# Unit 0's angles moved ahead of unit 1's gates, part of the gate arithmetic on other engines, and a new set of due times, in a gated linear attention with routed experts

## The chip, the cores and the metric

One core of one Trainium2 chip runs the whole program. The metric is the device time of one execution in microseconds. A profiled execution gives the trace; its span is what lies between the program's first and last instruction. The engines are named as in the profile: PE (TensorE matmuls), PEld (its weight loads), DVE (VectorE), ACT (ScalarE), POOL (GpSimd) and SP (the queue that issues most DMAs).

## The reference

The first half is a linear attention with a complex gate, over B = 4 batches, H = 8 heads, S = 768 positions, D = 48, all in float32:

```python
mag = np.sqrt(a_re * a_re + a_im * a_im)
scale = np.minimum(mag, 0.999) / (mag + 1e-06)
a_re_n, a_im_n = (a_re * scale, a_im * scale)
for t in range(S):
    ar, ai = (a_re_n[:, :, t, :, None], a_im_n[:, :, t, :, None])
    new_re = ar * S_re - ai * S_im
    new_im = ar * S_im + ai * S_re
    kv = np.einsum('bhd,bhe->bhde', k[:, :, t], v[:, :, t])
    S_re, S_im = (new_re + kv, new_im)
    y[:, :, t] = np.einsum('bhd,bhde->bhe', q[:, :, t], S_re)
```

The second half takes y as 3072 rows of 384, chooses the best of 8 experts for each row with `w_gate`, and gives each row its gate value times `relu(x @ w1[e]) @ w2[e]`.

## The kernel before

**Units and batches.** The sequence is cut into six units of 128 positions, which lie on the partitions. A unit has four batches; the loop `for g in range(NT)` runs over the 24 pairs (unit, batch). A half is two of a unit's four batches.

**The gates of a unit** become a decay and an angle. `gate_steps` makes four steps of the data `ar`, `ai`: `s0` a lower bound (a ScalarE Relu, or a VectorE maximum where `c<unit>` is true) and Ln; `s1` Exp, the ratio `ai*R` (L222), its clipping (L223) and its square (L224); `s2` Ln and a sum; `s3` Exp and the final log decay. `decay` sums that over the positions with a triangular matmul (`csl`) and takes two exponentials, E and Ei, for q and for k. `angle` takes the arctangent, `turns` sums it with matmuls (`cst`) and reduces it to whole and broken turns (`fg`, L283 to L286), and `rotation` takes two sines (`CS`). For units 2 to 4, `angle` also adds the phase carried from the unit before, which goes through DRAM (`cd`, `carry`). `csl` and `cst` share one PSUM buffer (`psC`).

**Attention.** `products` forms `Qe = q*E`, `Ke = k*Ei` and from them Q and K of 96 columns a head. `scores` transposes K and Q on TensorE (`tp`), ScalarE copies them out (`kt`, `qt`), TensorE multiplies (`at`), VectorE masks (`am`). `outer` forms K'V (`dk`), `state` updates the state `G` on VectorE. `results` sums, in one PSUM tile `yt`, `am` times V and, for units after the first, `qt` times `G`; `evict` copies `yt` to `ys`, `finish` turns it back to rows (`xb`), writes `x` to DRAM (`xd`) and keeps the router's logits. After units 2, 4 and 5 `route` ranks the rows for the experts.

**Experts.** From about 271 us on the eight experts follow one after another, each with its gathered rows, two matmul chains and a scatter.

**Order.** Instructions are placed by a planner: `put(t, f)` gives what `f` emits a due time `t`, counted in batches (lower is earlier), and an engine's ready instructions go in by due time. The times stand in the table `WHEN`: `s1.0.2` is step 2 of unit 1's part 0, `d` a decay, `a` an angle, `t` turns, `r` a rotation, `w` a group of `warm` matmuls (of no use to the result, they keep TensorE running), `p<n>` how many of unit n+1's gate steps are traced ahead of unit n's sine table. Unit 0 is done in three parts: batch 0, batch 1, batches 2 and 3.

**Two ScalarE tables.** Ln and Exp need one table, arctangent and sine the other. `table` loads one (`LE<n>`, `TR<n>`, about 1.28 us) and is ordered behind every table function traced since the last load, and every later one behind it. In the kernel before, unit 1's steps 0 and 1 are traced ahead of TR0 and its arctangent under TR0 too; the last two steps of unit 0's part 2 and unit 1's steps 2 and 3 follow LE1, and with them all four steps of unit 2.

**Loads.** SP issues the gates of unit 0, then those of unit 1, then q, k and v of unit 0's first half, then those of its second half.

Of the kernel before, what the change touches and what calls it, by code (L numbers as in the profile page):

```python
# [12 lines left out]
AF = mybir.ActivationFunctionType  # L13
# [25 lines left out]
def kernel(  # L39
# [123 lines left out]
    def warm(n):  # L163

        w = psX.tile([P, P], FP, tag="xb", padded_shape=[P, 512], name="warm")
        for i in range(n):
            ins = mm(w, tri, tri)
            if i == 0:
                tc.add_manual_dep(ins.ins, T["act"].ins.name, SYNC, reason="pace")
# [36 lines left out]
    def gate_steps(u, b0, b1):  # L206
# [13 lines left out]
        def s1():  # L220
            act(out=R, in_=ar, func=AF.Exp, scale=-1.0)
            tt(out=ai, in0=ai, in1=R, op=OP.mult)  # L222
            ts(out=ai, in0=ai, scalar1=-T_MAX, scalar2=T_MAX, op0=OP.max, op1=OP.min)  # L223
            T["act"] = nc.scalar.activation(out=R, in_=ai, func=AF.Square)  # L224
# [83 lines left out]
    def products(u, b, alone=False):  # L308
        half, c = divmod(b, HB)
        for nm, src, dec in (("Q", "q", "E"), ("K", "k", "Ei")):  # L310
            if c == 0:
                T[nm + "e"] = ch.tile([P, HB * H, D], FP, tag=nm + "e", name=nm + "e", bufs=1)
            if c == 0 or alone:
                sl = slice(c, c + 1 if alone else HB)
                tt(
# [7 lines left out]
            tt(out=t, in0=T["CS", u, half][:, hs], in1=bc(T[nm + "e"][:, hs], 2, 2), op=OP.mult)  # L323
# [28 lines left out]
    def results(u, b, hg):  # L352
        half, c = divmod(b, HB)
        V = T["v", u, half][:, c]
        for hp in range(2 * hg, 2 * hg + 2):
            o = [yt[i * 64 : i * 64 + D, hp] for i in range(2)]
            for i in range(2):
                mm(o[i], V[:, 2 * hp + i], T["am", u, b, hg][:, 2 * (hp % 2) + i], True, u == 0)
            for i in range(2):
                if u > 0:  # L360
                    mm(o[i], T["G", b][0:DD, 2 * hp + i], T["qt", u, b, hg][0:DD, 2 * (hp % 2) + i], False, True)
# [369 lines left out]
    def put(t, f, *a):  # L731
# [5 lines left out]
        "l1": 0, "l2": 1, "p0": 2, "p1": 4, "p2": 4, "p3": 2, "p4": 4, "p5": 3, "s0.0.0": -8.68, "c0": True,  # L737
        "w0": -2.82, "s0.1.0": -7.5, "s0.2.0": -5.29, "s0.0.1": -10.26, "w1": -3, "s0.1.1": -8.3, "s0.2.1": -3.21,
        "s0.0.2": -9.64, "w2": -3, "s0.1.2": -6.91, "s0.0.3": -6.55, "w3": -3, "s0.1.3": -6.6, "h1": True,
        "s1.0.0": -2.81, "c1": False, "s1.1.0": -4.38, "s1.0.1": -4.06, "s1.1.1": -3.59, "d0.0": -3.18, "d0.1": -1.67,  # L740
        "TR0": -3, "a0.0": -3.0, "a0.1": -2.9, "a0.2": -2.8, "t0.0": -2.5, "r0.0": -0.4, "p.0": -1.18, "t0.1": -0.55,
        "r0.1": -1.55, "p.1": -0.32, "t0.2": -1.22, "r0.2": -1.0, "a1": -1.69, "LE1": -1.01, "s0.2.2": -0.84,
        "s0.2.3": -0.8, "d0.2": -0.76, "s1.0.2": -3.39, "s1.1.2": -3.19, "s1.0.3": -2.99, "s1.1.3": -2.79,
        "d1.0": -2.33, "d1.1": -1.18, "h2": False, "s2.0.0": -5.0, "c2": False, "s2.0.1": -6.37, "s2.0.2": -4.19,
        "s2.0.3": -6.99, "TR1": -1.69, "t1.0": -1.85, "r1.0": -1.59, "t1.1": -0.53, "r1.1": 0.42, "a2": -4.5,
        "results0": 1.02, "results1": 1.04, "state": 1.61, "evict": 1.11, "scores0": -0.86, "scores1": 0.42,
        "outer": 0.43, "finish": 1.53, "products": -1.42, "LE2": -6.28, "d2.0": -3, "d2.1": 0.0, "h3": False,
        "s3.0.0": -4.87, "c3": False, "s3.0.1": -4.47, "s3.0.2": -3.47, "s3.0.3": -2.7, "TR2": -1.9, "t2.0": -2.5,
        "r2.0": -3.02, "t2.1": -1.45, "r2.1": 0.68, "a3": -3.28, "LE3": -4.96, "d3.0": -2.87, "d3.1": -1.87,
        "h4": False, "s4.0.0": -7.27, "c4": False, "s4.0.1": -7.25, "g2": -3.01, "TR3": -2.37, "t3.0": -2.37,  # L750
        "r3.0": -1.87, "t3.1": -2.78, "r3.1": -0.87, "a4": -4.45, "LE4": -3.65, "s4.0.2": -7.47, "s4.0.3": -6.41,
        "d4.0": -2.54, "d4.1": -1.42, "h5": False, "s5.0.0": -6.32, "c5": False, "s5.0.1": -7.01, "s5.0.2": -6.74,
        "s5.0.3": -6.62, "TR4": -1.22, "t4.0": -2.13, "r4.0": -0.31, "t4.1": -0.56, "r4.1": 0.83, "a5": -6.92,
        "LE5": -5.71, "d5.0": -3.39, "d5.1": -1.51, "g4": -2.93, "TR5": -3.13, "t5.0": -2.34, "r5.0": -2,
        "t5.1": -2.31, "r5.1": -1,
# [40 lines left out]
    for i in range(4):  # L796
        for j, h, c0, c1 in PARTS[: 3 if i < 2 else 2]:
            put(when(f"s0.{j}.{i}"), st[j][i])
            put(when(f"w{i}"), warm, 4)
# [3 lines left out]
    for j, h, c0, c1 in PARTS[:2]:  # L803
        put(when(f"d0.{j}"), decay, 0, h, c0, c1)
    put(when("TR0"), table, TR)
    for j, h, c0, c1 in PARTS:
        put(when(f"a0.{j}"), angle, 0, h * HB + c0, h * HB + c1)
    for j, h, c0, c1 in PARTS:
        put(when(f"t0.{j}"), turns, 0, h, c0, c1)
        put(when(f"r0.{j}"), rotation, 0, h, c0, c1)  # L810
        if h == 0:
            put(when(f"p.{j}"), products, 0, j, True)
    if STEPS[0] > 1:
        ANG[1] = True
        put(when("a1"), angle, 1, 0, B)
    put(-1, load_gates, 2, 0, B)

    def log_exp(n):
        X = n * B
        put(X + when(f"LE{n}"), table, LE)  # L820
        if n == 1:
            put(when("s0.2.2"), st[2][2])
            put(when("s0.2.3"), st[2][3])
            put(when("d0.2"), decay, 0, 1)
# [423 lines left out]
```

## Time and profile before

| | |
|---|---|
| median of 8 runs | 548.78 us (546.4 to 550.61) |
| the profiled execution | 548.87 us |
| its span | 547.1 us |
| TensorE's mean granted clock | 0.992 |
| busy: PE, PEld, DVE, ACT, POOL | 520.0, 370.8, 289.1, 214.4, 137.1 us |
| last `ys` copy of the attention | 269.97 us |

A timeline row has start, duration, engine, line, operation, what it writes and reads, and in brackets the idle time before it with what ended it. A row of a stretch has, for each engine, the busy time and, in brackets, the number of instructions; then the granted clock, the DMA engines' share and GB/s. Matmuls overlap one another and their ends are modelled, so busy PE is an upper reading. Some matmul records can be missing.

### The profile page before, as it was taken

The page shows a single profiled execution, that of the slowest core. Times are in us where ns is not written, and L with a number is a line of the kernel's source. Part 1 is how long each engine was busy: PE and PEld are TensorE (multiplying, and loading weights), DVE is VectorE, ACT ScalarE, POOL GpSimd, SP SyncE. Part 2 cuts the span into 40 slices and gives each one's busy share as a digit, 9 for nine tenths or more (in the row PEclk, how much of TensorE's full clock was granted, in tenths as well). Part 3 has the DMA queues.
Part 4 walks back from the last instruction along what each step waited for, and adds up shares of the span by engine and source line. Part 5 has one row for each costly group of instructions (what it writes and reads, how often), then busy time and mean ns, then how long its engine had stood idle before and what let it go on. Part 6 is the DMA issues. An engine that isn't in the chain of part 4 may idle for free.

```text
span 547.1 us, 8306 instructions
## 1 busy us (share of the span) xinstructions
PE 520.0 (95%) x3154; PEld 370.8 (68%) x3154; DVE 289.1 (53%) x585; ACT 214.4 (39%) x323; POOL 137.1 (25%) x161
## 2 busy tenths in 40 slices
PE   3879979999999999999999999999999999999996
PEld 2766868877888889898885755555555555565663
DVE  5378698687788888797284421241352413111210
ACT  6777888877658974563310010110201111000000
POOL 3000000000000000000127577772735622722101
PEclk9989989999999999999999999999999999999999
DMA  9987782768555944810818997555965543741001
GB/s 165 187 112 100 120 119 41 143 107 161 101 91 90 175 73 82 153 18 31 289 53 310 275 260 153 164 201 114 324 151 176 172 108 118 165 145 57 27 2 42
DMA packets 167735, 73.49 MB, mean 134 GB/s; under 512 B 149053, under 2 KB 160343, under 8 KB 167688
## 3 DMA queue, kind: packets, MB, share of 16 engines
q1 hardware_dynamic: 162792, 63.12, 53.8%
q0 software_dynamic: 4896, 9.77, 6.0%
q8 instruction: 27, 0.44, 0.4%
q14 instruction: 20, 0.16, 0.1%
HBM read 63.34 MB, written 9.73 MB: 134 GB/s over the span
## 4 chain that ended last, share of the span: by engine, by line
PE 81%; DMA 5%; DVE 4%; ACT 3%; issue 2%; POOLq 0%; SPq 0%; DVEq 0%; ACTq 0%
PE hps L69 23%; PE yps L69 22%; PE tp L332 7%; PE yt L69 7%; PE at L69 7%; PE dk L69 4%; PE cst L69 4%; PE xb L69 3%; PE csl L69 2%; DMA xd<-x 2%; DMA xg<-xd,tok 1%; DMA carry<-cd 1%; PE sp L69 1%; DVE fg L283 1%; DMA out_dram<-y,row 1%
## 5 line engine op out<-in xcount | busy, mean ns | idle before, releaser
L69 PE MATMUL yps<-wb,ht 128*128 128x384 f32 (+6 forms) x464 | 134.1, 487 | 0.0
L69 PE MATMUL hps<-xt,wa 128*128 128x416 f32 (+7 forms) x432 | 132.9, 466 | 0.0
L616 POOL DMA_INDIRECT xg<-xd,tok x92 | 97.8, 1063 | 97.9 <-PE tp L332 40.4
L69 PEld LDWEIGHTS hps<-xt,wa 128*128 128x128 f32 x432 | 79.8, 190 | 50.0 <-issue 24.2
L69 PEld LDWEIGHTS yps<-wb,ht 128*128 128x128 f32 (+6 forms) x464 | 75.1, 175 | 55.8 <-issue 8.6
L686 ACT ACTIVATE ht<-hps 128x416 f32<-128x416 f32 (+7 forms) x36 | 16.8, 467 | 149.5 <-PE hps L69 138.3
L708 DVE TENSOR_SCALAR y<-yps,gate 128x384 f32<-128x384 f32 (+1 forms) x23 | 14.2, 616 | 92.7 <-PE yps L69 92.7
L261 POOL DMA_DIRECT2D ai<-cd x4 | 3.4, 839 | 211.4 <-DMA cd<-carry 101.0
L69 PE MATMUL at<-qt,kt 96*128 96x128 f32 x384 | 53.9, 280 | 0.7 <-DVE am L340 0.7
L688 DVE TENSOR_SCALAR ht<-hps 128x416 f32<-128x416 f32 (+7 forms) x36 | 18.9, 525 | 66.2 <-PE hps L69 66.2
L655 POOL DMA_INDIRECT out_dram<-y,row x28 | 30.6, 1092 | 92.2 <-issue 42.0
L69 PEld LDWEIGHTS at<-qt,kt 96*128 96x128 f32 x384 | 47.7, 192 | 4.5 <-issue 1.1
L69 PE MATMUL yt<-am,v 128*48 128x128 f32 x384 | 42.8, 281 | 0.6 <-DVE am L340 0.6
L340 DVE TENSOR_TENSOR am<-at,tri 128x512 f32<-128x512 f32 x48 | 33.0, 687 | 18.6 <-PE at L69 18.5
L69 PE MATMUL yt<-qt,G 96*48 96x128 f32 x320 | 35.7, 274 | 0.0
L718 ACT COPY z<-yps 32x384 f32<-32x384 f32 (+3 forms) x13 | 6.1, 470 | 73.5 <-PE yps L69 73.4
L332 PE MATMUL tp<-ident,K 128*96 128x128 f32 x192 | 33.5, 285 | 1.2 <-DVE K L323 0.9
L69 PEld LDWEIGHTS dk<-v,K 128*96 128x96 f32 x320 | 32.9, 168 | 2.1 <-issue 1.0
L69 PE MATMUL dk<-v,K 128*96 128x48 f32 x320 | 33.5, 244 | 0.2 <-DVE G L371 0.2
L332 PE MATMUL tp<-ident,Q 128*96 128x128 f32 x192 | 33.4, 277 | 0.0
L334 ACT COPY kt<-tp 96x512 f32<-96x512 f32 x48 | 27.9, 581 | 11.0 <-PE tp L332 10.9
L69 PEld LDWEIGHTS yt<-am,v 128*48 128x48 f32 x384 | 24.4, 122 | 8.1 <-DVE am L340 2.0
(170 smaller groups left out, 670.8 us busy)
## 6 DMA issues: line engine op xcount, KB each, us to landing
wb<-in_moe_w_dram SPq DMA_DIRECT2D x8, 1536.0 KB
wa<-in_moe_w_dram SPq DMA_DIRECT2D x28, 384.0 KB, 6.8
q<-in_q_dram SPq DMA_DIRECT2D x12, 384.0 KB, 6.7
k<-in_k_dram SPq DMA_DIRECT2D x12, 384.0 KB
v<-in_v_dram SPq DMA_DIRECT2D x12, 384.0 KB, 6.3
xd<-x SPq DMA_DIRECT2D x24, 192.0 KB, 2.3
rc<-in_a_re_dram SPq DMA_DIRECT2D x6, 768.0 KB, 4.5
rc<-in_a_im_dram SPq DMA_DIRECT2D x6, 768.0 KB
```

The source lines that it names most:

```text
L69: T["mm"] = nc.tensor.matmul(o, lhsT=lhsT, rhs=rhs, start=start, stop=stop, skip_group_check=True)
L261: nc.gpsimd.dma_start(out=T["ai", u][0:1, b0:b1].rearrange("p b h d -> p (b h d)"), in_=cd[1, u - 1 : u, b0 * DM : b1 * DM], accum_op=OP.add,)
L283: ts(out=r, in0=cs[:, c0:c1], scalar1=MAGIC, scalar2=MAGIC, op0=OP.add, op1=OP.subtract)
L332: nc.tensor.transpose(out=tp[0:DD, j], in_=X[:, hg * 4 + j], identity=ident)
L334: nc.scalar.copy(out=t[0:DD], in_=tp[0:DD])
L340: tt(out=am, in0=at, in1=bc(tri, 1, 4), op=OP.mult)
L616: nc.gpsimd.indirect_dma_start(out=T["xg", i][0:n, j * w : (j + 1) * w], out_offset=None, in_=view, in_offset=bass.IndirectOffsetOnAxis(ap ...
L655: ins = nc.gpsimd.indirect_dma_start(out=out, out_offset=bass.IndirectOffsetOnAxis(ap=row[0:n, i, t : t + 1] if to is None else to[0:n], a ...
L686: nc.scalar.activation(out=ht[:, f, c0:c1], in_=ps, func=AF.Relu)
L688: T["held"] = ts(out=ht[:, f, c0:c1], in0=ps, scalar1=0.0, scalar2=None, op0=OP.max)
L708: ts(out=y[0:n], in0=ps[0:n], scalar1=g, scalar2=None, op0=OP.mult)
L718: nc.scalar.copy(out=z[j * w : j * w + n], in_=ps[j * w : j * w + n])
```

## The change

- `p0` goes from 2 to 0: unit 1's steps 0 and 1 and its arctangent are no longer traced ahead of TR0. All four steps follow LE1, and its arctangent follows TR1. The decays of unit 0's first two parts are due before the arctangents.
- `p1` goes from 4 to 2: unit 2's steps 2 and 3 are traced after LE2 instead of ahead of TR1. `c2` turns true: unit 2's lower bound is a VectorE maximum.
- In unit 0 the product `ai*R` of parts 1 and 2 and the squares of parts 0 and 2 go to GpSimd; the square of part 1 goes to VectorE. The square of part 0, 1 and 2 was ScalarE's.
- In unit 0 `Ke` goes from VectorE to GpSimd.
- `results` first multiplies with the state and then with V. The first matmul into each half of the partitions starts the sum for the whole tile.
- `warm` matmuls are paced by other instructions too (sines, the first `Q` products) and have counts of their own: 51 in place of 40.
- LE1 is placed right behind unit 0's rotations, ahead of its first `products`.
- Nearly all due times are new; for units 3 to 5 they are shifts of a few tenths for the most part. `h5` turns true: unit 5's gates are done in two halves.

```diff
-    def warm(n):
+    def warm(n, pace):
...
-                tc.add_manual_dep(ins.ins, T["act"].ins.name, SYNC, reason="pace")
+                tc.add_manual_dep(ins.ins, pace.ins.name, SYNC, reason="pace")
...
         def s1():
             act(out=R, in_=ar, func=AF.Exp, scale=-1.0)
-            tt(out=ai, in0=ai, in1=R, op=OP.mult)
+            pool = u < 2 and T["when"](f"m{u}.{b0}")
+            (nc.gpsimd.tensor_tensor if pool else tt)(out=ai, in0=ai, in1=R, op=OP.mult)
             ts(out=ai, in0=ai, scalar1=-T_MAX, scalar2=T_MAX, op0=OP.max, op1=OP.min)
-            T["act"] = nc.scalar.activation(out=R, in_=ai, func=AF.Square)
+            e = T["when"](f"q{u}.{b0}")
+            if e == "A":
+                T["act"] = nc.scalar.activation(out=R, in_=ai, func=AF.Square)
+            else:
+                (tt if e == "D" else nc.gpsimd.tensor_tensor)(out=R, in0=ai, in1=ai, op=OP.mult)
...
-                tt(
+                (nc.gpsimd.tensor_tensor if u < 2 and T["when"](f"e{u}{nm}") else tt)(
                     out=T[nm + "e"].rearrange("p (b h) d -> p b (h d)", b=HB)[:, sl],
...
-        for hp in range(2 * hg, 2 * hg + 2):
-            o = [yt[i * 64 : i * 64 + D, hp] for i in range(2)]
-            for i in range(2):
-                mm(o[i], V[:, 2 * hp + i], T["am", u, b, hg][:, 2 * (hp % 2) + i], True, u == 0)
-            for i in range(2):
-                if u > 0:
-                    mm(o[i], T["G", b][0:DD, 2 * hp + i], T["qt", u, b, hg][0:DD, 2 * (hp % 2) + i], False, True)
+        o = {(hp, i): yt[i * 64 : i * 64 + D, hp] for hp in range(2 * hg, 2 * hg + 2) for i in range(2)}
+        for G in (True, False) if u > 0 else (False,):
+            for hp, i in o:
+                j = 2 * (hp % 2) + i
+                if G:
+                    ws = T["G", b][0:DD, 2 * hp + i], T["qt", u, b, hg][0:DD, j]
+                else:
+                    ws = V[:, 2 * hp + i], T["am", u, b, hg][:, j]
+
+                new = hp == 0 and (u == 0 or G)
+                mm(o[hp, i], *ws, new, u == 0 or not G)
+                if new:
+                    T["new", i] = T["mm"]
+                else:
+                    behind(T["mm"], [T["new", i]])
...
-        "l1": 0, "l2": 1, "p0": 2, "p1": 4, "p2": 4, "p3": 2, "p4": 4, "p5": 3, "s0.0.0": -8.68, "c0": True,
+        "l1": 0, "l2": 1, "p0": 0, "p1": 2, "p2": 4, "p3": 2, "p4": 4, "p5": 3, "whole": 2, "s0.0.0": -9.96,
...
+        "q0.0": 'P', "w1": -10.16, "n1": 4, "s0.1.1": -8.6, "m0.1": True, "q0.1": 'D', "s0.2.1": -7.04, "m0.2": True,
+        "q0.2": 'P', "s0.0.2": -9.09, "s0.0.3": -8.92, "d0.0": -7.8, "w2": -7.5, "n2": 4, "w3": -6.4, "n3": 4,
+        "s0.1.2": -7.51, "s0.1.3": -6.65, "d0.1": -7.78, "TR0": -7.0, "a0.0": -6.36, "w4": -5.77, "n4": 4,
...
+        "w11": -1.45, "n11": 4, "LE1": -0.64, "s0.2.2": -0.2, "s0.2.3": -0.13, "d0.2": -1.61, "p.0": -5.1,
+        "e0Q": False, "e0K": True, "w7": -5.05, "n7": 2, "p.1": -5.0, "w8": -4.95, "n8": 1, "h1": True,
+        "s1.0.0": -3.7, "c1": False, "s1.1.0": -3.5, "s1.0.1": -3.6, "m1.0": False, "q1.0": 'A', "s1.1.1": -3.72,
...
-    for i in range(4):
-        for j, h, c0, c1 in PARTS[: 3 if i < 2 else 2]:
+    WHOLE = when("whole")
+
+    def parts_rest(j0, j1):
+        for i in (2, 3):
+            for j in range(j0, j1):
+                put(when(f"s0.{j}.{i}"), st[j][i])
+        for j, h, c0, c1 in PARTS[j0:j1]:
+            put(when(f"d0.{j}"), decay, 0, h, c0, c1)
+
+    def keep_warm(i, pace=None):
+        put(when(f"w{i}"), warm, when(f"n{i}"), T["act"] if pace is None else pace)
+
+    for i in range(2):
+        for j, h, c0, c1 in PARTS:
             put(when(f"s0.{j}.{i}"), st[j][i])
-            put(when(f"w{i}"), warm, 4)
+            if j == 0:
+                keep_warm(i)
+    for j in range(WHOLE):
+        parts_rest(j, j + 1)
+        if j == 0:
+            keep_warm(2)
+            keep_warm(3)
     if STEPS[0]:
         DONE[1] = STEPS[0]
         steps(1, 0, STEPS[0], 0)
-    for j, h, c0, c1 in PARTS[:2]:
-        put(when(f"d0.{j}"), decay, 0, h, c0, c1)
     put(when("TR0"), table, TR)
     for j, h, c0, c1 in PARTS:
         put(when(f"a0.{j}"), angle, 0, h * HB + c0, h * HB + c1)
+        keep_warm(4 + j)
     for j, h, c0, c1 in PARTS:
         put(when(f"t0.{j}"), turns, 0, h, c0, c1)
         put(when(f"r0.{j}"), rotation, 0, h, c0, c1)
-        if h == 0:
-            put(when(f"p.{j}"), products, 0, j, True)
+        keep_warm(9 + j)
...
+    put(when("LE1"), table, LE)
+    parts_rest(WHOLE, 3)
+    for j in range(2):
+        put(when(f"p.{j}"), products, 0, j, True)
+        keep_warm(7 + j, T["pace Q"])
     put(-1, load_gates, 2, 0, B)
 
     def log_exp(n):
         X = n * B
-        put(X + when(f"LE{n}"), table, LE)
-        if n == 1:
-            put(when("s0.2.2"), st[2][2])
-            put(when("s0.2.3"), st[2][3])
-            put(when("d0.2"), decay, 0, 1)
+        if n > 1:
+            put(X + when(f"LE{n}"), table, LE)
```

## The prediction

> **What bounds the kernel now.** I read the page's slices first, then the stretches, the timeline of ScalarE and TensorE up to 80 us, TensorE's waits, and the chain. In the page's slices each digit is a fortieth of the span, 13.7 us:
>
> ```profile
> PE   3879979999999999999999999999999999999996
> ACT  6777888877658974563310010110201111000000
> PEclk9989989999999999999999999999999999999999
> ```
>
> TensorE is full from the seventh slice on and half idle in the first, and the 8 and 7 of the next two are mostly its `warm` matmuls. So an early saving reaches the end only if TensorE gets real work sooner. The timeline (start, duration, what) shows when it does:
>
> ```profile
> 15.10 0.92 ACT L217 ACTIVATE R<-ar,a_low 128x768 f32<-128x768 f32 x1
> ...
> 23.92 1.28 ACT L181 ACT_TABLE_LOAD   x1
> ...
> 33.23 0.78 PE L332 MATMUL tp<-ident,K 128*96 128x128 f32 x4
> ...
> 38.15 1.28 ACT L181 ACT_TABLE_LOAD   x1
> ...
> 73.49 1.28 ACT L181 ACT_TABLE_LOAD   x1
> ...
> 78.58 1.09 PE L332 MATMUL tp<-ident,K 128*96 128x128 f32 x4
> ```
>
> These are: unit 1's first gate step; the load of the sine table, TR0, which stands behind all table functions traced before it; unit 0's first transposes; the load back, LE1; the next sine table, TR1; unit 1's first transposes. Next the stretches (busy us of PE, PEld, DVE, ACT, POOL; then granted clock, DMA share, GB/s):
>
> ```profile
> 0.00:10.00 10.00, 1.62 (x6) 1.35 (x6) 5.14 (x21) 5.08 (x9) 4.37 (x36) 1.00 1.07 157
> 10.00:20.00 10.00, 9.43 (x42) 7.67 (x43) 3.40 (x7) 7.80 (x14) 0.00 (x0) 1.00 1.45 187
> 38.10:73.50 35.40, 34.01 (x272) 27.16 (x273) 26.25 (x36) 28.72 (x40) 0.00 (x0) 1.00 0.63 92
> 78.00:82.00 4.00, 4.00 (x25) 3.36 (x23) 3.60 (x5) 3.50 (x5) 0.00 (x0) 0.58 1.46 187
> 80.00:105.20 25.20, 24.69 (x241) 21.76 (x239) 18.42 (x27) 21.97 (x29) 0.00 (x0) 0.97 0.51 79
> ```
>
> DMA runs at its rate from the start, and ScalarE has 6.7 us free between LE1 and TR1 and 3.2 us in the stretch after LE2. Last TensorE's longest waits (28 to 285 us) and, from the chain, the link that unit 2's angles hang on:
>
> ```profile
> PE csl L69 <- issue: 2.8, 1, 2.8
> ...
> PE yt L69 <- DVE am L340: 0.6, 2, 0.3
> ```
>
> ```profile
> 96.24 6.33 DMA carry<-cd
> ```
>
> The one large hole after 33 us is just ahead of unit 1.
>
> **The sum's base.** The profiled execution took 548.87 us, 547.1 of it span; the median of the eight runs, 548.78, is 0.1 below, so nothing is corrected for that.
>
> **Step 1, unit 0's first scores.** Unit 1's first two steps leave ScalarE's list ahead of TR0: eight operations of 0.84 to 0.93 us, 7.0 together, and the 3.0 us of waits between them. The first half's decay, due after them until now, moves ahead, so TR0 can load at about 16. Arctangents (0.52, 0.52, 0.85), `cst` 0.9, VectorE's three operations 1.5 and two sines 1.1 bring part 0's sines to about 20.5. Now q and k decide: 157 GB/s for 10 us and 187 after that move the gates of units 0 and 1 and half of q, 3.54 MB, by 20.5, and k's half by 22.6; both loads stay where they were. I allow 0.4 for the signal, an estimate. Ke is now GpSimd's. No row shows a two-input operation there: the 128x384 product is bounded by VectorE's row, 0.55, and by eight of the POOL copies of 128x48 (0.213), 1.70. I take three of the 128x128 AFFINE_SELECT (0.283), the row nearest in size: 0.85, and 1.7 for 128x768. With K at 0.95 and 0.5 of signals the first transposes come at 25.3 (24.5 to 27) instead of 33.2.
>
> The squares and two products of unit 0 on GpSimd and VectorE cost nothing here: with the upper price for part 0's square and part 1's product, 1.7 each for 0.5, the sines come 2.3 later, about when K does. Without that cover, had q come sooner, it would be those 2.3. The 51 `warm` matmuls (40 before) run ahead of the transposes; the set paced by part 2's sine could stand in TensorE's queue ahead of them and hold them 2 us, which step 3 hides.
>
> **Step 2, LE1.** It stands behind part 2's sines. VectorE has 7.3 us from 21 on (Qe 2x0.55, Q and K 4x0.95, part 2's turns 2.45); with the turns about half way, they end near 25.5, and sines of 0.93 and 0.85 bring LE1 to 27.5 instead of 38.15. Bounds: 25 with the turns first, 31.5 if Ke at 1.7 twice holds VectorE.
>
> Here a rule speaks against the change. No row has POOL and VectorE at work on data together past 5.2 us. The Trainium skill's page SBUF — State Buffer, section "SBUF: two separate sides", says that a GpSimd operation that reads SBUF and a VectorE one with two SBUF inputs exclude each other for the whole instruction. By it Ke's 0.85+0.85 on GpSimd would be lost to VectorE, and LE1 would come 1.7 later; the forecast would be 542.8.
>
> **Step 3, LE1 to TR1.** Now 35.3 us, 28.7 busy. Unit 1's eight operations come in (7.0, 6.4 without their overlaps), and two of the four score copies that preceded LE1 (1.1). Out go unit 2's Relu (1.58, now VectorE's maximum) and its second Ln and Exp (1.49, 1.58), moved past LE2, with their two waits on VectorE of 1.1 and 0.8. That makes 31.5 busy, less overlaps 30.7. Bounds: no idle time, 30.7; all of today's 6.7, 37.4. I take 33, with a third of that idle time, since the two waits make up most of another third. TR1 at 60.5, for 73.5.
>
> **Step 4, TR1 to unit 1's transposes.** Now 5.1, because unit 1's arctangents ran under TR0. Moved behind TR1, everything follows in a row: table 1.28, arctangent 1.47, eight `cst` 2.65, VectorE 0.95+0.95+0.55, sines 1.77, Q and K 1.8; 11.4, less 0.3 of overlap 11.1. Unit 1 starts at 27.5+33+11.1 = 71.6 instead of 78.6: **7.0 earlier**.
>
> TensorE's own work cannot bind before that: at the rates of the chain (eight `at` 0.89, eight `tp` 0.88, sixteen `dk` 1.32, eight `xb` 0.87, eight `yt` 0.5, eight `cst` or `csl` 2.6) unit 0's four batches need 4x6.7 and the sums left of units 0 and 1 some 9, 36 us from 25.3 on, that is until 61.
>
> **Step 5, clock.** After the hole at 74.1 to 76.9 the clock was 0.58 for 4 us: eight transposes took 1.77 against 0.88, sixteen `dk` 1.78 against 1.32, 1.4 together. The new order leaves TensorE some 10 us idle before 71.6, so I take half of that as **gained, 0.7** (0 to 1.4). The Trainium skill's page TensorE: Matmul & The Clock Gate, section "What's actually happening", puts the drop after an idle window of about 3.4 us; here a hole of 2.8 was followed by it, so the row goes ahead. By the rule shorter holes are free, the gain 1.4 and the forecast 540.4.
>
> **Step 6, the state's products first.** Same matmuls, and TensorE has work while VectorE masks. Its visible waits for `am` are 0.6, its weight loads' 1.0: **0.5** (0 to 1.6).
>
> **Step 7, what comes later.** Unit 2's Ln and Exp, 3.1, now stand after LE2; the 3.2 free there take most: **minus 0.4** (0 to -3.1). Due times of units 3 to 5 change order alone, with TensorE busy 39.9 of 39.9 us in unit 3: 0 (-2 to +2). From attention's end on all is driven by its last rows and moves along. On SP's queue unit 2's `ai` load (34.45 now, held by `cst`) only comes sooner.
>
> Sum: 7.0 + 0.7 + 0.5 - 0.4 = 7.8; 548.87 - 7.8 = **541.1 us**.
>
> **Rivals.**
>
> *More of it (534.1).* LE1 at 25, no idle time to TR1: unit 1 at 25+30.7+11.1 = 66.8, 11.8 earlier, with 1.4 and 1.6 of steps 5 and 6. For it: TR1 no longer hangs on unit 2's chain through VectorE. Against it: ScalarE would have to be full for 30 us, which it is in no stretch of that length.
>
> *The carry takes it (544.5).* Unit 2's `cst` waits for unit 1's last phases through DRAM, the 6.33 us link above. They now leave VectorE at 76.8; then, with one PSUM buffer for both halves, at 60.5+1.28+1.47+2.65+1.9 = 67.8 and, after 2.65+1.9 more, 72.4: only 4.4 earlier. Against it: SP issues them 4 and 9 us after that today, so there is slack to lose.
>
> *Slower (551.5): the gates behind LE1 do not fit.* Unit 1's steps no longer use ScalarE while q and k load; they share it with unit 0's copies. It decides at TR1: later than 67.5 (78.6-11.1), and unit 1 starts later than today. With Ke at 1.7 LE1 comes at 31.5; with all of today's idle time TR1 comes at 68.9 and unit 1 at 80.0, 1.4 late, and 1.2 of step 7 is uncovered. For it: the 6.0 us of step 4 are sure. Against: it takes both upper bounds.
>
> **How the numbers follow.** The sum 0.47 (its own range 537 to 545), the carry 0.18, more 0.20, slower 0.15. The range, 533.5 to 549.5, leaves out the outer half of "more" and most of "slower". Within 0.3% (1.6 us), about what a measurement of this kernel can tell from no change, falls 0.06, 0.04 from the weak end of the carry and 0.02 from the mild end of "slower"; faster 0.47+0.20+0.14 = 0.81, slower 0.13.
>
> **What would show it.** First transposes near 25, LE1 near 27.5, TR1 near 60, unit 1's transposes near 72, the last `ys` copy near 262 instead of 270, TensorE full after that. TR1 past 67.5 would prove steps 2 or 3 wrong; TR1 near 60 with attention's end unmoved, step 7.

## The result, and the profile after

The kernel after takes **553.69 us** (median of 12 runs, 552.28 to 555.49); the kernel before, over 33 runs shared with it, 548.24 (545.60 to 552.51). The ratio is **1.0098, 95% interval 1.0074 to 1.0122**: slower by 1%, where 541.1 was forecast. The profiled execution has a span of 552.7 us, 5.6 more than before.

The page's slices of the kernel after (a digit is a fortieth of the span, 13.8 us):

```profile
PE   5788999979999999999989999999999999999996
ACT  5578977668649957474310010110101101000000
PEclk9989999999999999999999999999999999999999
```

The first slice of PE is fuller (5 for 3), which is `warm` matmuls; the 7 of the sixth slice is gone, and one stands in the ninth, 111 to 124 us, where before there was a 9; an 8 in the twenty-first, 276 to 290 us, is new too. That is the result in small. The timeline of ScalarE and TensorE has the landmarks of the prediction (start, duration, what, and in brackets the idle time before it):

```profile
16.68 1.28 ACT L181 ACT_TABLE_LOAD   x1
...
29.47 0.64 PE L339 MATMUL tp<-ident,K 128*96 128x128 f32 x4 [2.85 <-DVE K L328]
...
32.95 1.28 ACT L181 ACT_TABLE_LOAD   x1
...
62.96 1.28 ACT L181 ACT_TABLE_LOAD   x1
...
74.25 0.64 PE L339 MATMUL tp<-ident,K 128*96 128x128 f32 x4 [0.43 <-DVE K L328]
...
80.03 1.28 ACT L181 ACT_TABLE_LOAD   x1
...
111.34 1.28 ACT L181 ACT_TABLE_LOAD   x1
...
121.89 2.44 PE L69 MATMUL csl<-ar,tri 128*128 128x384 f32 x4 [2.83 <-issue]
124.12 1.06 PE L339 MATMUL tp<-ident,K 128*96 128x128 f32 x4
...
273.93 0.59 ACT L392 COPY ys<-yt 128x512 f32<-128x512 f32 x1 [2.48 <-PE yt L69]
```

These are TR0, unit 0's first transposes, LE1, TR1, unit 1's first transposes, LE2, TR2, a `csl` of unit 3, unit 2's first transposes and the last `ys` copy. The prediction does not show the loads LE2 and TR2 of the kernel before; they are:

```profile
79.98 1.28 ACT L181 ACT_TABLE_LOAD   x1
...
105.24 1.28 ACT L181 ACT_TABLE_LOAD   x1
```

Read as legs (start to start, us), with unit 2's first transposes ("K2") at the end:

| | LE1 | LE1 to TR1 | TR1 to LE2 | LE2 to TR2 | TR2 to K2 | K2 | last `ys` of unit 1 | last `ys` of all |
|---|---|---|---|---|---|---|---|---|
| before | 38.1 | 35.3 | 6.5 | 25.3 | 14.4 | 119.6 | 117.3 | 270.0 |
| after | 33.0 | 30.0 | 17.1 | 31.3 | 12.8 | 124.1 | 114.5 | 273.9 |

TR1 comes 10.5 us sooner, unit 1's transposes 4.3 sooner (74.25 for 78.58). But **LE2 stands at 80.0 in both kernels**, TR2 comes 6.1 later, unit 2's transposes 4.5 later. Unit 1's last results come 2.9 sooner, so that 9.6 us lie between them and unit 2's transposes, 2.3 before. Nothing after that wins the time back: the last `ys` copy is 4.0 late.

The stretches (PE, PEld, DVE, ACT, POOL; clock, DMA share, GB/s) from start to unit 0's, unit 1's and unit 2's first transposes; three rows of before, then three of after:

```profile
0.00:33.20 33.20, 20.76 (x92) 15.29 (x93) 17.39 (x40) 22.41 (x34) 4.37 (x36) 0.95 1.25 167
33.20:78.60 45.40, 40.78 (x322) 32.56 (x320) 35.95 (x47) 37.83 (x50) 0.00 (x0) 0.99 0.70 106
78.60:119.60 41.00, 39.41 (x367) 33.85 (x367) 31.27 (x45) 32.71 (x42) 1.07 (x1) 0.97 0.64 106
```

```profile
0.00:29.50 29.50, 17.69 (x101) 14.88 (x101) 18.03 (x37) 15.20 (x25) 12.27 (x42) 1.00 1.29 174
29.50:74.20 44.70, 41.05 (x314) 33.65 (x314) 32.56 (x43) 39.23 (x52) 2.24 (x1) 0.96 0.63 95
74.20:124.10 49.90, 44.70 (x388) 35.51 (x389) 38.12 (x52) 36.10 (x46) 1.07 (x1) 0.98 0.76 128
```

ScalarE's column gives one account of this. By unit 2's transposes it has done 92.9 us of work before and 90.5 after; it sat idle 10.8 + 7.6 + 8.3 = 26.7 us before and 14.3 + 5.5 + 13.8 = 33.6 after. Work less 2.4, idle time more 6.9: 4.5 later. The gate steps taken out ahead of TR0 left 3.5 us more idle time there, while q and k load; their work came back behind LE1; and between units 0 and 1 its idle time shrank by 2.1, between units 1 and 2 it grew by 5.5. This says where the time lies, not yet what causes it.

TensorE's longest waits of after (28 to 290 us):

```profile
PE tp L339 <- DVE K L328: 4.6, 3, 2.8
PE csl L69 <- issue: 2.8, 1, 2.8
PE rk L69 <- DVE oh L430: 1.4, 1, 1.4
```

The hole of 2.8 in front of a `csl` is the one that stood at 74.1 before; it is now at 119.1, in front of unit 3's `csl`, which in TensorE's list stands ahead of unit 2's transposes. This `csl` starts at 121.89, when VectorE has just read unit 2's turns out of the buffer that `csl` and `cst` share (L289, 120.84 and 0.95 long). Unit 2's first K is ready at 122.66, so that the `csl` costs the transposes 1.5 us. Before, at that place, the transposes ran between two pairs of it:

```profile
118.95 0.83 PE L69 MATMUL csl<-ar,tri 128*128 128x384 f32 x2
119.62 0.60 PE L332 MATMUL tp<-ident,K 128*96 128x128 f32 x4
...
121.81 0.88 PE L69 MATMUL csl<-ar,tri 128*128 128x384 f32 x2
```

The rest of the 5.6 us is in the tail. Expert 1's first matmul comes at 303.6 for 299.0, expert 2's at 320.7 for 315.1: 4.6 and 5.6 late, of which 4.0 is the attention's. ScalarE's last copy of rows waits for a store:

```profile
ACT x L403 <- DMA xd<-x: 2.8, 1, 2.8
```

That was 0.6 before. The first expert's weights were issued 10.4 us ahead of the last `ys` before (259.6) and 8.3 after (265.6). That the store is late because it shares the DMA with them was not tested.

### The profile page after: what moved, and what is told of

Its sections match the earlier page's. It is cut to its first block, busy times and chain, and to the rows that moved or that the text cites. A ratio compares the mean times of both kernels' runs of the same rounds, so it can differ in the third digit from the quotient of the medians.

```text
span 552.7 us, 8353 instructions
## 1 busy us (share of the span) xinstructions
PE 522.4 (95%) x3176; PEld 373.9 (68%) x3176; DVE 291.8 (53%) x586; ACT 211.7 (38%) x325; POOL 149.4 (27%) x168
## 4 chain that ended last, share of the span: by engine, by line
PE 78%; DVE 6%; DMA 5%; issue 4%; ACT 4%; POOL 1%; POOLq 0%; SPq 0%; DVEq 0%; ACTq 0%
PE hps L69 21%; PE yps L69 20%; PE tp L339 8%; PE yt L69 7%; PE at L69 7%; PE dk L69 4%; PE xb L69 3%; PE csl L69 3%; PE cst L69 3%; DMA xd<-x 2%; DMA xg<-xd,tok 2%; POOL xg L631 1%; PE sp L69 1%; ACT R L175 1%; DVE fg L288 1%
## 5 line engine op out<-in xcount | busy, mean ns | idle before, releaser
L631 POOL DMA_INDIRECT xg<-xd,tok x92 | 101.0, 1098 | 101.7 <-DVE am L347 44.0
L69 PE MATMUL at<-qt,kt 96*128 96x128 f32 x384 | 55.1, 284 | 0.8 <-ACT qt L341 0.8
L703 DVE TENSOR_SCALAR ht<-hps 128x416 f32<-128x416 f32 (+7 forms) x36 | 18.9, 526 | 67.6 <-PE hps L69 67.5
L670 POOL DMA_INDIRECT out_dram<-y,row x28 | 29.5, 1053 | 89.4 <-issue 39.7
L69 PE MATMUL yt<-am,v 128*48 128x128 f32 x384 | 37.8, 277 | 0.6 <-DVE am L347 0.6
L341 ACT COPY kt<-tp 96x512 f32<-96x512 f32 x48 | 27.8, 578 | 22.0 <-PE tp L339 21.6
L69 PEld LDWEIGHTS dk<-v,K 128*96 128x96 f32 x320 | 33.6, 167 | 1.2 <-issue 0.7
L69 PE MATMUL yt<-qt,G 96*48 96x128 f32 x320 | 32.7, 280 | 0.0
L339 PEld LDWEIGHTS tp<-ident,K 128*96 128x96 f32 x192 | 21.1, 133 | 13.0 <-issue 5.7
```

Source lines behind the costliest of these rows:

```text
L69: T["mm"] = nc.tensor.matmul(o, lhsT=lhsT, rhs=rhs, start=start, stop=stop, skip_group_check=True)
L339: nc.tensor.transpose(out=tp[0:DD, j], in_=X[:, hg * 4 + j], identity=ident)
L341: nc.scalar.copy(out=t[0:DD], in_=tp[0:DD])
L631: nc.gpsimd.indirect_dma_start(out=T["xg", i][0:n, j * w : (j + 1) * w], out_offset=None, in_=view, in_offset=bass.IndirectOffsetOnAxis(ap ...
L670: ins = nc.gpsimd.indirect_dma_start(out=out, out_offset=bass.IndirectOffsetOnAxis(ap=row[0:n, i, t : t + 1] if to is None else to[0:n], a ...
L703: T["held"] = ts(out=ht[:, f, c0:c1], in0=ps, scalar1=0.0, scalar2=None, op0=OP.max)
```

## The experiments

Each ratio is to the kernel before in the same comparison, with its 95% interval. `WHEN` lines show only the keys changed. "ke_vector" is the kernel after with `Ke` back on VectorE; it became the base of most others.

**1. GpSimd's Ke, unit 2's gate steps, the later due times, the state's products: one at a time.**

```diff
-  "e0K": True                       # ke_vector: the kernel after, but
+  "e0K": False
```

> The change with Ke of unit 0 on VectorE again. Theory C (GpSimd's Ke holds VectorE: two Q products took 3.42 us beside it, against 0.95 each in the kernel before): the first transposes come at 27 to 28 instead of 29.5, LE1 at 31 instead of 32.95, and if the head still decides the end, the time falls by 1 to 2 us. Theory A or B (the loss is made at unit 2): LE1 earlier just the same, the end within 1 us of 553.7.

Measured: 550.67 us, **1.0043 [1.0016, 1.0070]**: between this ratio and 1.0098 lie 3.0 of the 5.4 us, and they go with this one word. The trace shows how. VectorE in the kernel after, then in ke_vector, and GpSimd in the kernel after:

```profile
24.27 3.42 DVE L328 TENSOR_TENSOR Q<-CS,Qe 128x768 f32<-128x768 f32 x2
```

```profile
24.26 1.82 DVE L328 TENSOR_TENSOR Q<-CS,Qe 128x768 f32<-128x768 f32 x2
26.00 1.02 DVE L320 TENSOR_TENSOR Ke<-k,Ei 128x384 f32<-128x384 f32 x2
```

```profile
24.08 2.79 POOL L320 TENSOR_TENSOR Ke<-k,Ei 128x384 f32<-128x384 f32 x2 [7.30 <-ACT CS L175]
42.99 2.24 POOL L320 TENSOR_TENSOR Ke<-k,Ei 128x768 f32<-128x768 f32 x1 [16.12 <-ACT Ei L175]
```

Beside GpSimd's two products VectorE's two take 3.42 instead of 1.82, 1.60 more than they take alone; doing both `Ke` itself costs VectorE 1.02. The transposes come at 28.0 without GpSimd and at 29.5 with it, unit 2's at 121.5 and 124.1. LE1 did not move (33.1 without GpSimd, 33.0 with it), though 31 was expected: what holds LE1 is not GpSimd.

```diff
-  "p1": 2                           # p1_four: the kernel after, but
+  "p1": 4
```

> The change with p1 = 4: all four gate steps of unit 2 are traced ahead of TR1 again, with their due times unchanged; everything else as in the change. Theory A (unit 2's last Ln and Exp, moved past LE2, stretch the stretch from LE2 to TR2 from 25.3 to 31.3 us, so that unit 2 starts 4.5 us late): TR2 comes back from 111.3 to 105 to 108, unit 2's first transposes from 124.1 to below 121, the time falls by 3 us or more from 553.7. Theory B (the other due times, above all the later products): within 1 us of 553.7.

Measured: 562.38 us, 1.0241 [1.0165, 1.0317]. With unit 2's last two gate steps ahead of TR1 again and unit 1's gates still behind LE1, LE1 to TR1 is 38.0, and TR1 to LE2 21.6 with ScalarE busy 11.1 of it: after TR1 unit 1's arctangent, turns and sines follow in a row, and ScalarE waits between them. Moving those two steps behind LE2 is needed in this order, not a fault of it: without it the kernel is 8 us slower by the ratios.

```diff
-  "s3.0.0": -4.65, "TR4": -0.88, "products": -0.74, "p1": 2, "c2": True, "h5": True, ...
+  "s3.0.0": -4.87, "TR4": -1.22, "products": -1.42, "p1": 4, "c2": False, "h5": False, ...
                                     # late_old: the kernel after, but units 2 to 5 as before
```

> The change with the head kept (all due times and choices of units 0 and 1, GpSimd, the order of results) but the due times and choices that belong to units 2 to 5 as in the kernel before, with p1 = 4, c2 and h5 false, and products due at -1.42 again. If the head is a gain and the loss lies in the later times (A and B together): 4 us below the kernel before, 544 to 546. If the head itself costs: 550 or more.

Measured: 561.88 us, 1.0244 [1.0190, 1.0298], the same as p1_four. It has `p1` = 4 as well, so that it says no more than that the other due times do not mend p1_four.

```diff
-  for hp in ...: V's products of a pair, then G's products of it
+  for G in (True, False): for hp, i in o: ...
                                     # before_state_first: the kernel before, but
```

> The kernel before with only the order of results changed (state's products first, one start for the tile). Theory D (this order costs, since the first product of the next batch must wait for the copy of the tile before anything else): 550 or more. Otherwise 547 to 549, since TensorE's visible waits for the mask are 0.6 us in all.

Measured: 547.46 us, 0.9987 [0.9959, 1.0014]: 0.7 by the medians, not to be told from nothing.

**2. Within ke_vector: later due times, products, turns, engines.**

```diff
  # ke_late_times: ke_vector with units 2 to 5 and "products" as before (p1 stays 2)
  # ke_products:   ke_vector with "products": -1.42 for -0.74
  # ke_turns_first: ke_vector with "t0.2": -5.3, "r0.2": -5.2 for -4.24, -2.07
  # ke_all_old_engines: ke_vector with unit 0's products on VectorE, its squares on ScalarE
```

> The change with Ke on VectorE (run ke_vector, 550.7), and the due times of units 2 to 5 and of the products as in the kernel before; p1 = 2, c2 and the head as in the change. Theory E (the later due times, products above all, are what makes unit 2 late; the two runs with p1 = 4 stood 50.3 and 44.0 us between the first transposes of units 1 and 2, with new and old later times): that distance falls from 48.1 to 43 to 45 and the time to 545 to 547.5. If the distance stays at 47 or more, the late start of unit 2 comes from the two steps moved past LE2 and the time stays within 1.5 of 550.7.

Measured: 551.53 us, 1.0070 [1.0040, 1.0100]. Taking back the due times of units 2 to 5 brings nothing; in this set they are not the cause.

> The change with Ke on VectorE and only the due time of products as in the kernel before (-1.42 for -0.74). Theory E, if products alone carry it: as good as ke_late_times, 545 to 548. If it is the spread of the other times: within 1 us of ke_vector's 550.7.

Measured: 551.35 us, 1.0094 [1.0063, 1.0124]; nor is that of the products.

> The change with Ke on VectorE and the turns and sines of unit 0's part 2 due ahead of the first products (t0.2 -5.3, r0.2 -5.2 for -4.24 and -2.07). Theory F (LE1 at 33 instead of the 27.5 that I forecast, because VectorE does those turns after the products): LE1 at 28.5 to 30, TensorE's work done by 60 us up by 1 us or more, and if the head decides the end, 547 to 549. If the head does not decide it, 550 to 551.5.

Measured: 559.09 us, 1.0225 [1.0189, 1.0261]. This is the forecast's own wish: part 2's turns ahead of the products. LE1 then comes at 30.4, but the first transposes also come at 30.4 (28.0 in ke_vector), TR1 at 67.2, and TensorE has a hole of 4.8 us at 66.7. An early LE1 bought with late products costs 8 us by the medians.

> The change with all of unit 0's squares and products back on ScalarE and VectorE (no arithmetic on GpSimd). Theory C, if the early part on GpSimd also costs (VectorE's sum at 13.0 us took 1.77 instead of 0.55 beside GpSimd's product of 1.81): TR0 at 16 or sooner, time 549 to 550.5. If the early squares are a gain: TR0 after 17, 551 or more.

Measured: 553.29 us, 1.0103 [1.0075, 1.0131]; LE1 at 35.3 for 33.1. So in the new order the early squares and products on GpSimd and VectorE are a gain, by the medians 2.6 us.

**3. Unit 1's gates put back.**

```diff
  # gates_back_ahead:    ke_vector with "p0": 2 for 0
  # one_gate_step_back:  ke_vector with "p0": 1 for 0
  # before_squares_moved: the kernel before with the state's products first and the
  #                      m0.*, q0.* choices (products, squares) of the change
  # ke_unit5_whole:      ke_vector with "h5": False
```

> ke_vector, with unit 1's first two gate steps (Ln and Exp, eight ScalarE operations of 0.84 to 0.93 us) traced ahead of TR0 again and its arctangent under that table, as before the change; all due times as in the new order. Theory G (the moved gate steps had filled ScalarE's waiting time while q and k load, and come back in the stretch from 33 to 60 us where ScalarE is nearly full): ScalarE is idle less ahead of 30 us, TR0 at 23 to 25, unit 1's transposes not later than 78, last ys copy at 269 to 271, time 547 to 549 against 550.7 for ke_vector. The forecast's theory (an early TR0 and LE1 are worth their whole advance): LE1 and everything after it 5 to 7 us later than in ke_vector, 554 to 558.

Measured: 551.12 us, 1.0064 [1.0042, 1.0085]. Neither theory holds: the forecast's 554 to 558 does not come, nor G's 547 to 549. The first transposes are 6.4 us later than in ke_vector and unit 2's at the same 121.4, as the stretches say:

```profile
0.00:34.40 34.40, 19.71 (x101) 16.38 (x102) 19.68 (x42) 21.70 (x32) 9.47 (x40) 0.90 1.19 161
34.40:74.60 40.20, 39.34 (x316) 32.10 (x313) 30.45 (x41) 31.88 (x44) 0.00 (x0) 1.00 0.64 99
74.60:121.40 46.80, 43.44 (x390) 36.25 (x389) 35.94 (x51) 37.22 (x47) 1.07 (x1) 0.96 0.68 121
```

ScalarE's idle time is 12.7 + 8.3 + 9.6 = 30.6 us; in ke_vector it is 30.7. What unit 0 gains by going first, 6.4 us, is worth nothing at unit 2, and filling the time of loading again brings nothing either.

> ke_vector, with only the first of unit 1's gate steps (two Ln halves, some 3.4 us of ScalarE) ahead of TR0. Theory G: TR0 near 20, still ahead of q's landing, so that the first transposes move by less than 1 us and 3 us of work leave the stretch from 33 to 60; time 547.5 to 549.5. The forecast's theory: unit 0's angles 3.5 us later, TR1 no earlier than in ke_vector, 551 to 554.

Measured: 549.90 us, 1.0042 [1.0012, 1.0073], the same as ke_vector. The first transposes moved by 3.9 us, not by less than 1, and still the time is the same.

> The kernel before with two parts of the change alone: the state's products ahead of the values' products, and unit 0's part 0 square and part 2 square and product on GpSimd, part 1's product on GpSimd and square on VectorE; order and due times as before. Theory G: the table TR0 still waits for unit 1's gate steps, which now come sooner by the ScalarE time taken away (three squares, 0.5 to 0.9 us each): 545.5 to 547 against 546.8 to 548.2 for before. Rival (GpSimd's longer operations hold up VectorE and the gate steps behind them): 548 to 551.

Measured: 549.00 us, 1.0025 [0.9997, 1.0054]. In the old order the early squares bring the first transposes 0.3 us (32.4 for 32.7 in before_state_first): ScalarE only waits longer there. The runs' mean granted clock is 0.981 to 0.993, that of before mostly 0.994 to 0.997.

> ke_vector, with unit 5's gates taken whole instead of by halves, as before the change. Theory: the halves put more and smaller operations on ScalarE between 190 and 230 us, where TensorE is full, so nothing changes: 550 to 551.5. Rival (the halves delay TR4 and with it units 4 and 5): 548.5 to 549.5, with the last ys copy 1 us or more sooner than 271.6.

Measured: 551.84 us, 1.0072 [1.0046, 1.0098]: unit 5's halves do no harm.

**4. Unit 2's start and the tail.**

```diff
  # gates_of_both_ahead:    ke_vector with "p0": 2, "p1": 4
  # unit3_steps_later:      ke_vector with "p2": 2 for 4
  # last_rows_own_buffer:   ke_vector; the last batch's x takes the tile of Ke, free by then
  # unit3_later_own_buffer: both of the last two
  # gates_ahead_late_old:   gates_of_both_ahead with the later due times of before
  # before_own_buffer:      before_state_first, the last batch's x as above
```

> ke_vector, with the gates of both units traced ahead as before the change: unit 1's first two steps ahead of TR0 and all four of unit 2's ahead of TR1; the due times stay the new ones. Theory H (the time between unit 1's last results and unit 2's first transposes, 2.3 us before, 8.6 in ke_vector, is what eats the head's gain, and it is long because unit 2's last two gate steps and its decay stand between LE2 and TR2): that gap falls to 2 to 4 us, but unit 1 starts at 78 to 80 as before; last ys copy 269 to 271, time 547 to 550. Rival (the new due times of units 2 to 5 cost the time whatever the order): gap 6 us or more, 551 to 555.

Measured: 553.18 us, 1.0083 [1.0047, 1.0119]. The gap is 5.7 us: smaller than 8.6, though not the 2 to 4 of theory H, and the time is not smaller.

> ke_vector, with only the first two of unit 3's four gate steps ahead of TR2 (a 1.5 us Ln and a 1.6 us Exp move behind LE3). Theory H: TR2 comes 3 us sooner than 108.5, unit 2's first transposes at 118 to 119 instead of 121.5, the gap of 8.6 shrinks to 5 to 6 and the last ys copy comes at 268 to 270; time 547 to 549. Rival (TR2 is held by TensorE's sums for unit 2's decay, not by ScalarE's queue, or the steps moved delay unit 3 as much): TR2 within 1 us of 108.5, 550 to 552.

Measured: 553.43 us (4 runs), 1.0111 [1.0052, 1.0170]. TR2 comes at 110.2, not 3 us sooner than 108.5: ScalarE's queue does not hold it, and theory H falls in that form. The gap still shrinks to 6.5, and the time does not fall with it.

> ke_vector, with the last batch's output rows copied into a buffer that is free by then, instead of one whose store to DRAM is still under way (ScalarE's last x copy waits 2.8 us for that store, 0.6 in before). Theory: the ranks of the last tokens come 2 to 2.5 us sooner, the first 256-row matmuls of expert 1 1 to 2 us sooner, time 548.5 to 549.8. Rival (the gather behind it waits for the stores anyway): 550.2 to 551.2.

Measured: 550.73 us, 1.0061 [1.0029, 1.0093], no gain over ke_vector. ScalarE's copy now goes ahead,

```profile
272.07 0.48 ACT L409 COPY x<-xb 128x384 f32<-128x384 f32 x1 [1.23 <-PE xb L69]
```

1.8 us after the last `ys` instead of 5.4, and expert 1 begins 28.1 us after it instead of 29.6; but another wait stands in its place, here within expert 1 (at 299.8) and in the next run ahead of expert 2 (at 315.9):

```profile
PE hps L69 <- DVE xt L671: 0.5, 1, 0.5
```

```profile
PE hps L69 <- DVE xt L654: 1.5, 1, 1.5
```

> Both edits before this at once, unit 3's last two gate steps behind LE3 and a buffer of its own for the last rows. Theory H and the tail's theory add: 545 to 547.5, at least as fast as before. If either falls, 548 to 551.

Measured: 550.92 us, 1.0066 [1.0043, 1.0089]: expert 1 begins at 298.3 for 300.2 in unit3_steps_later, expert 2 at 315.9 for 316.6. The two edits do not add up to the 545 to 547.5 of theory H.

> gates_of_both_ahead, with the due times and choices of units 2 to 5 and of the products taken back too. What is left of the change: unit 0's and unit 1's due times, the warm matmuls and their paces, the early squares and products, the state's products first. Theory I (with the gates of both units ahead, the later units' new due times are what costs: TR2 at 112.2 there, 105.2 before): TR2 at 104 to 107, last ys copy 268 to 270, time 546 to 549. Rival J (units 0 and 1's own due times and the halved clock windows of the head cost it): 550 to 553, with a granted clock below 0.99 in most runs.

Measured: 557.91 us, 1.0178 [1.0139, 1.0216]. Theory I falls, by 8 us and more: with the gates of units 1 and 2 ahead as before and the later due times as before, all that is left of the change is units 0 and 1's due times, the `warm` matmuls and the small edits, and this is 10 us slower than before. Of that rest, the early squares and the state's products cost nothing clear in the old order (before_squares_moved). Rival J was right in direction and too low.

> The kernel before, with the state's products first and the last batch's output rows in a buffer of their own. Of the 0.6 us that ScalarE's last x copy waits there for a store, and of the 0.5 expected of the state's products, 0.5 to 1.5 us together should be gained: 546 to 547.5 against 547.4 to 548.2 for before, ratio 0.997 to 0.999, faster than both kernels. Rival (the rows that come sooner wait for expert 2's turn on VectorE, as in last_rows_own_buffer): ratio 0.999 to 1.001.

Measured: 547.67 us, 0.9987 [0.9963, 1.0011]. No version here is shown faster than the kernel before.

**The legs of all of them together** (us):

| | LE1 | LE1 to TR1 | TR1 to LE2 | LE2 to TR2 | K2 |
|---|---|---|---|---|---|
| before and its three variants | 37.4 to 38.3 | 35.3 | 6.5 | 25.2 to 25.3 | 117.9 to 119.6 |
| ke_vector | 33.1 | 29.0 | 17.9 | 28.5 | 121.5 |
| ke_late_times | 33.1 | 29.1 | 18.5 | 29.2 | 120.3 |
| one_gate_step_back | 37.0 | 27.7 | 17.6 | 28.1 | 121.7 |
| gates_back_ahead | 39.5 | 25.0 | 13.5 | 29.4 | 121.4 |
| gates_of_both_ahead | 39.4 | 34.4 | 5.9 | 32.5 | 121.9 |
| gates_ahead_late_old | 39.3 | 35.9 | 5.9 | 34.0 | 126.1 |
| p1_four | 32.9 | 38.0 | 21.6 | 33.3 | 137.0 |

Two things stand out. A short leg from LE1 to TR1 is paid for from TR1 to LE2: the two make 41.8 before, 45 to 48 where unit 1's arctangent stands behind TR1 (58 to 60 in ke_turns_first, late_old and p1_four), 38.5 to 41.8 where it ran under TR0. And LE2 to TR2 is 25 us in each of the four kernels with the old due times of units 0 and 1, and 27 to 34 in all sixteen with the new ones, whatever is done about gates or later units. With the old ones the last thing ahead of TR2 is unit 3's gate step; with the new ones it is mostly the second half of unit 2's decay (in the kernel after, E at 109.42 and Ei at 110.49, against 101.3 and 102.9 before).

K2 is known to no better than about 3 us: ke_unit5_whole and last_rows_own_buffer have ke_vector's instructions up to there, with 17.9 and 28.5 us for TR1 to LE2 and LE2 to TR2, and their K2 is 118.7 and 119.3 for its 121.5. In ke_unit5_whole K2 and the last `ys` (268.5) even come before those of the kernel before (119.6 and 270.0), and its span is still 1.5 us longer: that loss lies behind the attention. So the longer leg goes with the new due times, but that it is what costs ke_vector its time is not shown.

**What stays open:** where the 2.4 us (by the ratio) between ke_vector and the kernel before come from. Part may be TensorE's granted clock. Of the 105 runs of before, 77 have a mean clock of 0.994 to 0.997 and a median of 547.1 us, 10 have 0.982 to 0.988 and 550.8. A straight line through all of them gives 0.44 us per 0.001. By this estimate the lower clock would go with 0.9 of the kernel after's 5.4 us (0.992 for 0.994), 0.6 of ke_vector's, but about 2.9 of the 3.5 us of unit3_later_own_buffer (0.987). No run tells whether the clock or the waits came first. Open too is why the second half's `csl` of unit 2, whose own due time is 0.0 in both sets, is placed so much later once units 0 and 1 have new due times. The planner sets it from all due times together, and apart from part 2's turns and sines in ke_turns_first no run changed those of units 0 and 1 one by one. How the `warm` matmuls share in it was not tried either. Nor did I follow how 0.8 us between ke_vector and the kernel after at unit 1 grow to 2.6 at unit 2, which is within the 3 us just named.

## Why the prediction was wrong, step by step

The forecast was 7.8 us of gain, the profile shows a loss of 5.6. Of the 13.4 between them, 2.7 are lost by the time unit 1 starts (4.3 sooner instead of 7.0, steps 1 to 4) and 10.7 behind that (steps 5 to 7). In cause, 3.0 us are GpSimd's `Ke` in place of VectorE's (ke_vector); the rest is traced below, but no single edit brings it back.

**Step 1 was mis-sized: 29.5, not 25.3 (24.5 to 27).** TR0 (16.7) and part 0's sines (done at 21.7 for 20.5) came about nearly as worked out (of the eight operations one, at 25.64, ran behind TR0 already), and k was not the limit: `Ke`, which reads it, started at 24.08. VectorE's queue was: part 1's turns until 23.4, two `Qe`, two `Q`, the first operation of part 2's turns, and only then K at 28.48. The working took the path of part 0's K alone and left out what stands ahead of it on its engine. In ke_vector, without GpSimd, that queue gives 28.0; GpSimd's `Ke` adds 1.5. GpSimd's price was 2.79 for two, above the 0.85 each that was taken, inside the bounds of 0.55 to 1.70.

**Step 2 failed: LE1 at 33.0, past the upper bound of 31.5.** "With the turns about half way" was a choice without a row. Part 2's turns begin at 27.61, behind the `Q` pair, and are broken by the `K` pair (28.48 to 30.29); what the first sine needs is done at 31.15, and it starts at 31.28, behind two copies that unit 0's transposes release. The rule that was set against the change agrees with the trace: the Trainium skill, page SBUF — State Buffer, section "SBUF: two separate sides", has a GpSimd operation that reads SBUF and a VectorE one with two SBUF inputs shut each other out for the whole instruction. Besides the 3.42 above, GpSimd's product of 12.54 to 14.35 holds a VectorE operation that takes 0.55 otherwise:

```profile
13.00 1.77 DVE L237 SCALAR_TENSOR_TENSOR ar<-ar,R 128x384 f32<-128x384 f32 x1 [1.36 <-ACT R L175]
```

It ends 0.42 after GpSimd's. The rule's 1.7 us, for which the forecast gave 542.8, came true as 1.60 on VectorE and about 3.0 at the end, but not where the forecast put it: LE1 is at 33.1 without GpSimd too.

**Step 3 failed in its work: LE1 to TR1 took 30.0, under the lower bound of 30.7 (33 forecast).** ScalarE was busy 26.0 us of it and idle 4.0; the forecast had 30.7 and 2.3. (Its terms add up to 31.5 with overlaps already taken off; taking them off again has no row.) The leg is shorter because work was left for later: two score copies, two `ys` copies, one `x` copy and unit 2's square. Before, all four of unit 0's `ys` copies come ahead of TR1, now two. The other two come after it, at 67.0 and 77.1; unit 0's last results are 6.6 us later than before.

**Step 4 was right: 11.3 from TR1 to unit 1's transposes, 11.1 forecast.** Step 2 lost 5.5 us and step 3's shorter leg gave 3.0 back, so unit 1 began 4.3 instead of 7.0 us sooner. But a start is not work done, since unit 0's last results were still to come, and the working ended here.

**Step 5: no gain.** The hole moved from 74.1 to 119.1 and the clock fell after it as before (half from 78.0 before, from 122.4 after, 3.41 us each). Over all runs the mean granted clock is 0.992 for after and 0.994 for before. The Trainium skill's page TensorE: Matmul & The Clock Gate, section "What's actually happening", puts the fall after an idle window of about 3.4 us; here the hole was 2.83, and some of the falls described at the end followed shorter ones.

**Step 6: 0.7 by the medians in before_state_first, interval across zero; 0.5 was forecast.** That neither confirms nor contradicts it.

**Step 7 is the step that turned the sign.** "Minus 0.4 (0 to -3.1)" was all it held for what comes behind LE2; the stretch from unit 1's to unit 2's transposes grew from 41.0 to 49.9, by 8.8. The step counted the work that moves there against free time (3.2 us after LE2), and that part was about right: ScalarE's busy time from LE2 to TR2 went from 21.97 to 23.75, 1.8 more.

```profile
80.00:111.30 31.30, 30.24 (x285) 24.59 (x286) 24.77 (x34) 23.75 (x32) 1.07 (x1) 1.00 0.58 109
```

Its idle time went from 3.2 to 7.6. Two things were never worked out: when LE2 comes, and where the other instructions' places in the queues go when the due times ahead of them change. LE2 is at 80.0 again because it waits for the sines of unit 1's second half. With the arctangent behind TR1 the second half's turns begin on VectorE only at 74.11, after the first half's products, and end at 77.86; LE2 comes 5.8 us after unit 1's first transposes, 1.4 before. Unit 0's last `ys` copy and a score copy, ahead of these sines on ScalarE, account for about 1 us of it. The working of step 4 followed this chain for the first half only. The range of 2 either way for "due times change order alone" was for units 3 to 5; units 0 and 1 had none. The tail was to move along with the attention's end and lost 1.6 more.

**The rivals.** "The gates behind LE1 do not fit" gave 551.5, nearest to the 553.7 measured. It named what the account of idle time shows, ScalarE's work taken out of the time of loading, but that this causes the loss is not shown: gates_back_ahead put the work back there and gained nothing. Its point of decision was wrong: TR1 at 63.0 is well short of 67.5, and the loss comes one unit later. "The carry takes it": unit 2's `cst` runs at 113.84, straight behind other work of TensorE and without a wait, while the last operation on `carry` ended on VectorE at 104.7; no time was lost to the carry there. "More of it" had unit 1 at 66.8; it was 74.25. The prediction's own last sign, TR1 early with the attention's end unmoved, came up (63.0, and the last `ys` 4.0 late), and pointed to step 7.

## What to carry to other kernels

Follow a saving at the start through to the first place where the bounding engine has nothing to do, and count the idle time of the engine that feeds it on the way: here ScalarE's work was 2.4 us less and its idle time 6.9 more. Such an account shows where the time lies; what to undo only a run can tell, and putting the steps back where ScalarE waits for loads gained nothing by itself. Before a product goes to GpSimd, ask what VectorE does at that moment: here VectorE lost 1.60 us beside two products that cost it 1.02 itself. In a plan in which all due times act together, a set of new times is one edit: parts of it taken back by themselves brought between 3 us of gain and 9 of loss here, and say little of what they would bring outside the set.

## What the runs showed of the hardware

A fall is a stretch at less than full clock in a trace's clock records. Every fall in these traces is to one half and lasts 3.41 us, 6.83 or, in p1_four, 10.24: once, twice or three times the same window (apart from the last one of a run, which its end cuts off). It came after holes as short as 1.9 us (41.5 to 43.4 in ke_vector, half clock from 43.2 for 6.83 us), and not after each of that length (13.0, 1.8 us, the same kernel). The stretches of full clock between two falls are whole multiples of the same 3.41 us as well (44.37 is 13 of them before, 88.75 is 26 after), so falls begin on a grid of this spacing. Whether a hole's place on the grid decides if a fall follows was not tested. Three kernels with the same legs behind TR1 show the price at that place: with no fall there LE1 to TR1 is 27.1 (last_rows_own_buffer), with one of 3.41 us 27.5 (ke_unit5_whole), with 6.83 us 29.0 (ke_vector). The mean clock differs between runs of one kernel: before takes 545.3 to 549.7 at 0.994 to 0.997, and 549.7 to 551.5 at 0.986 to 0.988.

GpSimd's two-input operations took, with 384 and 768 columns, 0.83 and 1.47 us for a square and 1.00 and 1.81 for a product; beside VectorE's products 2.24 for 768.
